# Top-k attention and Fourier mixing on one core: the seven products of the fast block multiply laid into two PSUM banks in turns

## The chip, the core and the metric

The kernel runs on one core of one Trainium2 chip. The metric is the device time of one execution in microseconds (us), as the median of several runs. The core's engines are TensorE (PE in the profile, its weight loads PEld), VectorE (DVE), ScalarE (ACT), GpSimd (POOL) and SyncE (SP, which issues the transfers here). Each engine works through its own list of instructions in order, and waits on semaphores where it needs another engine's result. TensorE writes its results to PSUM, which has eight banks of 128 x 512 float32; VectorE and ScalarE read them from there.

## The reference, cut to what matters

Eight batches, eight heads, 576 tokens, head size 64. The attention keeps the 32 largest scores of each row. Its output, 576 x 512 per batch, goes through a Fourier mix, a normalisation and two matrix products with 2048 hidden channels.

```python
scores = scale * np.matmul(q, k.transpose(0, 1, 3, 2))
kth = np.partition(scores, -top_k, axis=-1)[..., -top_k:-top_k + 1]
scores = np.where(scores >= kth, scores, -1000000000.0)
attn = softmax(scores)                       # cut: max, exp, sum + 1e-9
x = np.matmul(attn, v)                       # then (B,H,S,D) -> (B,S,H*D)

mixed = np.real(fft(fft(x, axis=1), axis=2)).astype(np.float32)
u = x + mixed
un = (u - mean(u)) / np.sqrt(var(u) + 1e-06) # over the last axis
ch = np.maximum(un @ w_ch1, 0.0) @ w_ch2
out = (u + ch).astype(np.float32)
```

## The kernel before

The program is one long loop over steps `i`. A step handles one tile of 128 query rows (36 steps per batch, 288 in all): TensorE makes scores for tile i + 3, transposes the finished tile i - 2 (`tpP`) and multiplies by `v`; VectorE finds the 32 largest of each row with MAX8 and MATCH_REPLACE8; GpSimd turns the 32nd value into bounds (`nt`); ScalarE and GpSimd mask (`wk`), and ScalarE takes the exponential. The mix and the matrix products of the batch before are cut into units and laid between these as TensorE filler: `hidden` units write `hp`, the products of the second matrix are called p1 to p7.

PSUM has four pools: two banks `ps_s` for scores, two `ps_t` for transposes, one `ps_o`, and three `ps_m` that `bank()` hands out in turn. A bank that is held is passed over.

```python
held, turn = set(), [0]
def bank(shape, name, hold=False):
    while turn[0] in held:
        turn[0] = (turn[0] + 1) % 3
    n = turn[0]
    turn[0] = (n + 1) % 3
    t = ps_m.tile(shape, F32, name=name, tag=f"m{n}", bufs=1)
    if not hold:
        return t
    held.add(n)
    return t, lambda: held.discard(n)
```

A bank that isn't held may be handed out while an earlier reader is still to come. TensorE then waits for this reader.

The Fourier mix has three TensorE parts for each batch: four token transforms (`yp`, two for each parity), five channel transforms (`mp`, one per tile of tokens) and five transposes (`tpu`). In all batches but the last they take a bank of the three:

```python
yp = ps_t.tile(shape, F32, name=name, tag="tp") if b == B - 1 else bank(shape, name)
...
mp = ps_s.tile(shape, F32, name=name, tag="sp") if b == B - 1 else bank(shape, name)
...
tp = ps_t.tile(shape, F32, name=name, tag="tp") if b == B - 1 else bank(shape, name)   # tpu
```

The second matrix product is done, for batches 1 to 7, as a block multiply with seven products instead of eight (two row tiles `ta`, `tb`, two halves of the channels), once for each of two chunks `ch` of tokens. Each product is two units of four matmuls of 256 columns. All share two banks, `v` and `w`, with a half (`lo`, `hi`) per result. A product that follows in the same half adds to what stands there. GpSimd makes the sums of blocks of the hidden layer (`mix`), each in two halves.

```python
def p2(part):
    if part == 0:
        mix("21", "21", "22", ALU.add)
    c = product("v", lo, "12", streamed(B21), part, True)
    if part: to_x(ta, lo, c, None if ch else 0)
def p4(part):
    c = product("v", hi, "22", streamed(T4), part, False)
    if part: to_x(tb, lo, c, None if ch else 1); banks["v"][1]()      # bank v given back
def p1(part):
    c = product("w", lo, "11", b11, part, True)
    if part:
        to_x(ta, lo, c, 2)
        mix("11", "21", "11"); mix("12", "12", "11"); mix("22", "22", "11")
def p5(part):
    need((b, ch, ("21", part)))
    c = product("w", hi, "21", streamed(T1), part, False)
    if part: to_x(tb, hi, c, 3)
def p6(part):
    need((b, ch, ("11", part)))
    c = product("w", lo, "11", streamed(T2), part, False)
    if part: to_x(ta, hi, c, 0)
def p3(part):
    need((b, ch, ("12", part)))
    c = product("w", hi, "12", b22, part, False)
    if part: to_x(ta, hi, c, 1); store(ta)
def p7(part):
    need((b, ch, ("22", part)))
    c = product("w", lo, "22", streamed(T3), part, False)
    if part: to_x(tb, slice(0, DM), c, None if ch else 2); store(tb); banks["w"][1]()
# order of the units: p2, p4, p1, p5, p6, p3, p7
```

`to_x` adds a result to `x`. With a place `n`, ScalarE scales it out of PSUM at once and GpSimd adds it later from a list `sums`; with `None`, or in the last batch, VectorE does both in one instruction (line 992). Outside the last batch that instruction is put off by one to two steps (`late_next`), so that it doesn't stand ahead of the top-k work.

GpSimd takes from `sums` once in each step, ahead of the bounds; `need` pulls everything that stands before a wanted key:

```python
run(i, "pool0")
some_sums(max(3.4 - planned, 0.0))      # us of sums in this step
bounds(i)
...
def need(key):
    while key not in summed:
        got, _, fn, _ = sums.pop(0)
        fn()
        summed.add(got)
```

Of the kernel before, what the change touches and what calls it, by code (L numbers as in the profile page):

```python
# [64 lines left out]
def kernel(  # L65
# [544 lines left out]
    def dft_tokens(b, par, g2):  # L610

        while any(u[2] == "hidden" for u in queue):
            one_unit()
        _, zw, fg = folded[b, par]
        if b not in y_of:
            y_of[b] = batp.tile([P, 4, S], F32, name=f"y_{b}", tag="y")
        y = y_of[b]
        shape, name = [P, 2, KQ], f"yp_{b}_{par}_{g2}"

        yp = ps_t.tile(shape, F32, name=name, tag="tp") if b == B - 1 else bank(shape, name)  # L620

        def mm(gg, st, lhsT, rows, table, start=False):

            nc.tensor.matmul(  # L624
                yp[0:rows, gg, :],
                lhsT=lhsT,
                rhs=fs[:, table, par, st, :],
                start=start,
                stop=st == 2,
                skip_group_check=True,  # L630
            )


        for gg in range(2):
            g = 2 * g2 + gg
            for st in range(3):
                f = fg[:, st] if st < 2 else ftail
                mm(gg, st, f[:, P * g:P * (g + 1)], P, gg, start=gg == 0 and st == 0)
        if g2 == 0:
            for st in range(3):  # L640
                mm(1, st, zw[:, st, Q1:Q1 + 1] if st < 2 else ftail[:, DM:DM + 1], 1, 0)

        mir, back = (
            (slice(HS + 2, S, 2), slice(KQ - 2, 0, -1)) if par == 0
            else (slice(HS + 1, S, 2), slice(KQ - 2, None, -1))
        )
        y2 = y[:, 2 * g2:2 * g2 + 2, :]
        nc.scalar.copy(out=y2[:, :, par:HS + 1:2], in_=yp[:, :, 0:KQ - par])
        nc.scalar.copy(out=y2[:, 0, mir], in_=yp[:, 0, back])
        nc.scalar.mul(out=y2[:, 1, mir], in_=yp[:, 1, back], mul=sg[:, g2:g2 + 1])  # L650
        if par == 1 and g2 == 1:
            tails_of_y(b)
        return 2.15
# [6 lines left out]
    def dft_channels(b, t, quick=False):  # L660

        rows, y = ROWS[t], y_of[b]
        shape, name = [P, 2, DM // 2], f"mp_{b}_{t}"
        mp = ps_s.tile(shape, F32, name=name, tag="sp") if b == B - 1 else bank(shape, name)
        for par in range(2):
            for j in range(2):
                g = 2 * par + j
                if t == 4:
                    lhsT = yt_of[b][:, g].rearrange("p h r -> p (h r)")
                else:  # L670
                    k0 = HS * (t // 2) + P * (t % 2)
                    lhsT = y[:, g, k0:k0 + P]
                nc.tensor.matmul(
                    mp[0:rows, par, :], lhsT=lhsT, rhs=fd[:, g, :],
                    start=(j == 0), stop=(j == 1),
                )
        if quick:
            xt = two(x_of[b][0:rows, t, :])
            at(now[0], "dve", lambda: nc.vector.tensor_tensor(
                out=xt, in0=mp[0:rows], in1=xt, op=ALU.add  # L680
            ))
            at(now[0], "dve", lambda: stats(b, t))
            return 1.75
        key = (b, t > 1 and t < 4)
        if key not in us_of:
            us_of[key] = batp.tile(
                [P, 2 if key[1] else 3, DM], F32, name=f"us_{b}_{t}", tag="fold_d" if key[1] else "fold_s"
            )
        us = us_of[key][0:rows, CHUNKS[int(key[1])].index(t), :]
        nc.scalar.copy(out=two(us), in_=mp[0:rows])  # L690
        return 1.75
# [35 lines left out]
    def channels_first(b, t):  # L727

        rows = ROWS[t]
        ch, col = CHUNK_OF[t]  # L730
        if (b, ch) not in unT_of:
            unT_of[b, ch] = batp.tile(
                [P, NDT, CW[0]], F32, name=f"unT_{b}_{ch}", tag="fold_s" if ch == 0 else "y"
            )
        shape, name = [P, NDT, P], f"tpu_{b}_{t}"
        tp = ps_t.tile(shape, F32, name=name, tag="tp") if b == B - 1 else bank(shape, name)
        for dt in range(NDT):
            nc.tensor.transpose(
                tp[:, dt, 0:rows], x_of[b][0:rows, t, P * dt:P * (dt + 1)], ident[0:rows, 0:rows]
            )  # L740
        nc.scalar.copy(out=unT_of[b, ch][:, :, col:col + rows], in_=tp[:, :, 0:rows])
        return 0.6

# [14 lines left out]
    stream = []  # L760
    for _ in range(B - 1):
        for ch in range(2):
            stream += [(o, kc) for o in (B21, T4, T1, T2, T3) for kc in range(NK)]
            if ch == 0:
                stream += [(o, kc) for kc in range(NK) for o in (T1, B21)]
    places = [w2[:, kc, DH:DM] for kc in range(NK)] + [w2[:, NK + kc, 0:DH] for kc in range(NK)]
# [57 lines left out]
            summed.add(key)  # L824

    def need(key):
        while key not in summed:
            got, _, fn, _ = sums.pop(0)
            fn()
            summed.add(got)  # L830

    def mlp_units(b):
# [110 lines left out]
        def fast(ch):  # L945
# [37 lines left out]
                for n in range(2):  # L983
                    later((dst, n), 1.25, lambda n=n: go(NK // 2 * n), True)

            def to_x(t, cols, src, n):

                xt = x[:, t, cols].rearrange("p (e c) -> p e c", c=DH)
                e = xt.shape[1]
                if n is None or last:  # L990
                    def add():
                        nc.vector.scalar_tensor_tensor(  # L992
                            out=xt,
                            in0=src.rearrange("p (e c) -> p e c", e=1).to_broadcast([P, e, DH]),
                            scalar=rs[:, t:t + 1], in1=xt, op0=ALU.mult, op1=ALU.add,
                        )
                    if last:
                        add()
                    else:
                        late_next.append(add)  # L1000
                    return
                r = room(n)
                nc.scalar.mul(out=r, in_=src, mul=rs[:, t:t + 1])
                key = "x", t, cols.start, n
                used[n] = b, ch, key
                rb = r.rearrange("p (e c) -> p e c", e=1)
                later(key, 0.75 * e, lambda: nc.gpsimd.tensor_tensor(
                    out=xt, in0=xt, in1=rb.to_broadcast([P, e, DH]) if e > 1 else rb, op=ALU.add
                ))

            def store(t):
# [7 lines left out]
                if last:  # L1019
                    go()  # L1020
                else:

                    later(("out", t), 0.0, lambda: at(now[0] + 2, "load2", go))

            def half_bank(name, cols):
                if name not in banks:
# [19 lines left out]
            def p2(part):  # L1046
                if part == 0:
                    mix("21", "21", "22", ALU.add)
                c = product("v", lo, "12", streamed(B21), part, True)
                if part:  # L1050
                    to_x(ta, lo, c, None if ch else 0)

            def p4(part):
                c = product("v", hi, "22", streamed(T4), part, False)
                if part:
                    to_x(tb, lo, c, None if ch else 1)
                    banks["v"][1]()

            def p1(part):
                c = product("w", lo, "11", b11, part, True)  # L1060
                if part:
                    to_x(ta, lo, c, 2)
                    mix("11", "21", "11")
                    mix("12", "12", "11")
                    mix("22", "22", "11")

            def p5(part):
                need((b, ch, ("21", part)))
                c = product("w", hi, "21", streamed(T1), part, False)
                if part:  # L1070
                    to_x(tb, hi, c, 3)

            def p6(part):
                need((b, ch, ("11", part)))
# [3 lines left out]

            def p3(part):
                need((b, ch, ("12", part)))  # L1080
                c = product("w", hi, "12", b22, part, False)
                if part:
                    to_x(ta, hi, c, 1)
                    store(ta)

            def p7(part):
                need((b, ch, ("22", part)))
                c = product("w", lo, "22", streamed(T3), part, False)
                if part:
                    to_x(tb, slice(0, DM), c, None if ch else 2)  # L1090
                    store(tb)
                    banks["w"][1]()

            def tails(half, part):
                n = CHUNKS[ch].index(4)
# [17 lines left out]

            units = [
                (1.75, lambda f=f, part=part: f(part), "back")
                for f in (p2, p4, p1, p5, p6, p3, p7) for part in range(2)
            ]
            if ch == 0:
                units += [
# [139 lines left out]
    for b in range(B):  # L1259
# [42 lines left out]
                at(ft[par], "pe1", lambda b=b, par=par, g2=g2: dft_tokens(b, par, g2), 2.15)  # L1302
        for n, t in enumerate((0, 1, 4, 2, 3)):
            quick = first or last
            s = fc + (0 if first else n // 3 if last else n // 2)
            at(s, "pe2", lambda b=b, t=t, q=quick: dft_channels(b, t, q), 1.75)
            if not quick:
                at(s, "pool2", lambda b=b, t=t: add_mixed(b, t))
# [50 lines left out]
    while i < N + 4 or plan or queue or sums:  # L1359
# [98 lines left out]

        planned = 1.5 * len(plan.get((i, "pool0"), [])) + 1.3 * len(plan.get((i, "pool2"), []))
        run(i, "pool0")  # L1460
        some_sums(max(3.4 - planned, 0.0))
        bounds(i)
        if i < PER_BATCH:
            mask(i)
        for fn in late_now:
# [44 lines left out]
```

## Time and profile before

| what | value |
|---|---|
| median of 3 runs | 1973.29 us (1973.12 to 1973.54) |
| span of the profiled run | 1971.8 us |
| VectorE busy | 1588.8 us (81%) |
| ScalarE busy | 1220.0 us (62%) |
| GpSimd busy | 961.9 us (49%) |
| DMA rate over the span | 77 GB/s, hardware queue 26.2% of 16 engines |

Busy is the time in which an engine has an instruction under way. An engine's idle time is put down to what ended it, for example "PE hp L848 <- DVE x L992": TensorE stood before a matmul into `hp` until a VectorE instruction of line 992 that works on `x` was done. "issue" means that the profile shows nothing that it waited for. The granted clock (PEclk) is the share of full TensorE clock that the chip allowed; at 0.5 a matmul takes twice as long.

### The profile page before, as it was taken

To read this page: it belongs to the slowest core of one execution; us is meant where nothing else is said; L and a number is where in the kernel's file an instruction comes from. 1 tells how busy PE (TensorE), PEld (TensorE's weight loads), DVE (VectorE), ACT (ScalarE), POOL (GpSimd) and SP (SyncE) were. 2 spreads that over 40 slices of the span, in tenths; PEclk is the share of its full clock that TensorE was granted. 3 is DMA by queue.
4 is the path that set the end of the run, shared out by engine and by line. 5 is a ranking of instruction groups with operands and counts; after the bars stand their busy time and mean duration, and the time that the engine had idled before them with its cause. 6 is when DMAs were issued, how large, how long until landed. Compare 5 with 4: busy or idle time off the path is not lost.

```text
span 1971.8 us, 30544 instructions
## 1 busy us (share of the span) xinstructions
PE 1803.6 (91%) x9520; PEld 1271.9 (65%) x9520; DVE 1588.8 (81%) x3274; ACT 1220.0 (62%) x3108; POOL 961.9 (49%) x1246
## 2 busy tenths in 40 slices
PE   5566799999999989999999998999799999998998
PEld 3333465465676766777666765767567776777777
DVE  8999989899999989888798877988868888852110
ACT  6878657676876767666676665666656667651100
POOL 4768544546434573546435563446525464344112
PEclk7787899999999999999999998999999999999999
DMA  5323001211224230333114131233203331133151
GB/s 162 111 87 97 19 13 51 86 40 29 62 65 135 62 93 19 105 92 97 50 40 146 52 96 34 82 107 83 66 18 112 86 98 53 46 118 107 43 163 43
DMA packets 235633, 151.37 MB, mean 77 GB/s; under 512 B 135248, under 2 KB 226512, under 8 KB 235472
## 3 DMA queue, kind: packets, MB, share of 16 engines
q1 hardware_dynamic: 234688, 149.22, 26.2%
q8 instruction: 76, 1.25, 0.3%
q14 instruction: 85, 0.70, 0.1%
q10 hardware_dynamic: 784, 0.21, 0.0%
HBM read 134.65 MB, written 14.68 MB: 76 GB/s over the span
## 4 chain that ended last, share of the span: by engine, by line
PE 69%; POOL 12%; DVE 8%; issue 5%; ACT 4%; DMA 0%; SPq 0%; POOLq 0%; DVEq 0%; ACTq 0%
PE hp L848 24%; PE cw L1036 10%; PE o L465 6%; PE sp L363 5%; PE tpP L428 5%; POOL wk L401 4%; PE cv L1036 4%; DVE m L384 3%; PE yp L624 3%; DVE wk L386 3%; PE cp L1105 3%; POOL w L215 2%; POOL w L214 2%; PE cp L872 2%; PE sp_t L333 1%
## 5 line engine op out<-in xcount | busy, mean ns | idle before, releaser
L401 POOL TENSOR_TENSOR wk<-S,wk 128x576 f32<-128x576 f32 x288 | 407.9, 1416 | 764.1 <-ACT wk L400 743.5
L384 DVE MAX8 m<-wk 128x8 f32<-128x576 f32 x864 | 623.0, 748 | 5.2
L848 PE MATMUL hp<-unT,w 128*128 128x256 f32 (+1 forms) x2048 | 544.9, 413 | 13.7 <-DVE x L992 11.6
L848 PEld LDWEIGHTS hp<-unT,w 128*128 128x128 f32 x2048 | 376.8, 192 | 140.4 <-issue 34.3
L386 DVE MATCH_REPLACE8 wk<-m,wk 128x576 f32<-128x576 f32 x576 | 427.5, 742 | 0.0
L1036 PE MATMUL cw<-w,hT 128*128 128x256 f32 x1056 | 256.6, 389 | 26.8 <-POOL hT L980 14.6
L407 ACT ACTIVATE wk<-wk,nt 128x576 f32<-128x576 f32 x288 | 224.7, 780 | 71.4 <-POOL wk L401 70.2
L400 ACT ACTIVATE wk<-S,nt 128x576 f32<-128x576 f32 x288 | 226.9, 788 | 48.5 <-POOL nt L393 47.4
L428 PE MATMUL tpP<-ident,wk 128*128 128x128 f32 x1152 | 183.9, 284 | 73.4 <-ACT wk L407 48.6
L1036 PEld LDWEIGHTS cw<-w,hT 128*128 128x128 f32 x1056 | 193.7, 192 | 72.8 <-issue 25.4
L384 DVE MAX8 m<-S 128x8 f32<-128x576 f32 x288 | 213.9, 743 | 24.1 <-ACT S L337 21.8
L852 ACT ACTIVATE hT<-hp 128x320 f32<-128x320 f32 (+1 forms) x256 | 105.0, 410 | 202.4 <-PE hp L848 200.4
L428 PEld LDWEIGHTS tpP<-ident,wk 128*128 128x128 f32 x1152 | 140.5, 145 | 136.1 <-ACT wk L407 70.1
L431 ACT COPY PT<-tpP 128x512 f32<-128x512 f32 (+1 forms) x320 | 171.1, 546 | 80.0 <-PE tpP L428 77.5
L386 DVE MATCH_REPLACE8 wk<-m,S 128x576 f32<-128x576 f32 x288 | 213.5, 741 | 0.0
L980 POOL TENSOR_TENSOR hT<-hT 128x512 f32<-128x512 f32 x112 | 140.7, 1272 | 124.8 <-ACT hT L852 95.7
L465 PE MATMUL o<-PT,v 128*64 128x256 f32 (+3 forms) x1440 | 195.9, 415 | 1.9 <-ACT PT L431 1.9
L366 ACT COPY S<-sp 128x512 f32<-128x512 f32 (+1 forms) x264 | 141.9, 589 | 49.7 <-PE sp L363 49.6
L363 PE MATMUL sp<-kT,qT 64*128 64x512 f32 (+1 forms) x528 | 159.0, 662 | 4.2 <-ACT means L1234 3.3
L465 PEld LDWEIGHTS o<-PT,v 128*64 128x64 f32 x1440 | 111.5, 153 | 72.2 <-issue 15.7
L1036 PE MATMUL cv<-w,hT 128*128 128x256 f32 x432 | 102.7, 382 | 1.2 <-DVE x L992 1.2
L1036 PEld LDWEIGHTS cv<-w,hT 128*128 128x128 f32 x432 | 78.4, 190 | 16.2 <-issue 4.3
(149 smaller groups left out, 2145.0 us busy)
## 6 DMA issues: line engine op xcount, KB each, us to landing
w<-w_parts SPq DMA_DIRECT2D x624, 128.0 KB, 2.5
space<-in_moe_w_ch_dram SPq DMA_DIRECT2D x32, 512.0 KB, 3.6
nat<-in_q_dram SPq DMA_DIRECT2D x128, 64.0 KB, 2.1
v<-in_v_dram SPq DMA_DIRECT2D x128, 64.0 KB, 2.1
out_dram<-x SPq DMA_DIRECT2D x32, 256.0 KB, 2.1
nat<-in_k_dram SPq DMA_DIRECT2D x124, 64.0 KB, 2.2
w_s<-w_parts SPq DMA_DIRECT2D x48, 128.0 KB, 2.6
w_parts<-w_t SPq DMA_DIRECT2D x8, 512.0 KB, 2.9
```

The costliest lines, as they stand in the source:

```text
L363: nc.tensor.matmul(sp[r], lhsT=qT[hd, q_cols], rhs=kT[hd, :], start=True, stop=True)
L366: nc.scalar.copy(out=s_t[r, keys], in_=sp[r])
L384: ops.append(lambda src=src, m8=m8: nc.vector.max(out=m8, in_=src))
L386: ops.append(lambda src=src, m8=m8: nc.vector.match_replace(w, m8, src, NEG))
L400: nc.scalar.activation(out=w, in_=Ssb[i], func=AF.Relu, scale=-FAR, bias=Nt[i][:, 1:2])
L401: nc.gpsimd.tensor_tensor(out=w, in0=Ssb.pop(i), in1=w, op=ALU.subtract)
L407: nc.scalar.activation(out=w, in_=w, func=AF.Exp, bias=Nt.pop(i)[:, 0:1], accum_out=den_t[pair % 3][:, c:c + 1],)
L428: nc.tensor.transpose(tp[:, c, :], p_sb[:, k0 + P * c:k0 + P * (c + 1)], ident)
L431: nc.scalar.copy(out=pt[:, NF * he:NF * (he + 1), col:col + w], in_=tp[:, :, o:o + w])
L465: nc.tensor.matmul(o[D * e:D * (e + 1), c0:c1], lhsT=vv[:, c, e, :], rhs=pt[:, 2 * NF if c == NF else NF * e + c, c0:c1], start=(c == 0), ...
L848: nc.tensor.matmul(hp[:, 0:w], lhsT=w1[:, dt, P * it:P * (it + 1)], rhs=unT[:, dt, 0:w], start=(dt == 0), stop=(dt == NDT - 1),)
L1036: nc.tensor.matmul(dst, lhsT=h()[a][:, kc, :], rhs=rhs, start=start and kc == 0, stop=kc == NK - 1, skip_group_check=True,)
```

## The change

It regroups the use of PSUM around the seven products, and moves some GpSimd work.

1. The products run in the order p2, p1, p5, p4, p6, p3, p7 and go to the banks v, w, v, w, w, v, w. Before, they went to v, v and then five times to w.
2. Both banks stay held until VectorE's last read of them is in the program: `to_x` takes a `then`, called once that read is emitted. Before, they were given back at once.
3. Of the results of a chunk, p3 and p7 go through VectorE; before it was p2, p4 and p7 in chunk 1 alone.
4. With two of three banks held for longer, half the transforms of batches 2 to 6 go to the two banks of `ps_t`: `yp` with g2 = 1, `mp` of tiles 1 and 2, `tpu` of tiles 0 and 2.
5. For the same batches the channel transforms are spread: one per step and not two.
6. GpSimd takes up to 2.1 us of sums before the bounds and 1.3 us after them; `need` pulls only sums of the wanted kind (mix, or add to x). Stores are planned one step earlier.

```diff
-        yp = ps_t.tile(shape, F32, name=name, tag="tp") if b == B - 1 else bank(shape, name)
+        there = b == B - 1 or b > 1 and g2 == 1
+        yp = ps_t.tile(shape, F32, name=name, tag="tp") if there else bank(shape, name)
...
-        mp = ps_s.tile(shape, F32, name=name, tag="sp") if b == B - 1 else bank(shape, name)
+        if b == B - 1:
+            mp = ps_s.tile(shape, F32, name=name, tag="sp")
+        elif b > 1 and t in (1, 2):
+            mp = ps_t.tile(shape, F32, name=name, tag="tp")
+        else:
+            mp = bank(shape, name)
...
-        tp = ps_t.tile(shape, F32, name=name, tag="tp") if b == B - 1 else bank(shape, name)
+        there = b == B - 1 or b > 1 and t in (0, 2)
+        tp = ps_t.tile(shape, F32, name=name, tag="tp") if there else bank(shape, name)
...
-            stream += [(o, kc) for o in (B21, T4, T1, T2, T3) for kc in range(NK)]
+            stream += [(o, kc) for o in (B21, T1, T4, T2, T3) for kc in range(NK)]
...
     def need(key):
-        while key not in summed:
-            got, _, fn, _ = sums.pop(0)
-            fn()
-            summed.add(got)
+        if key in summed:
+            return
+        kind = next(s[3] for s in sums if s[0] == key)
+        for s in [s for s in sums if s[3] == kind]:
+            sums.remove(s)
+            s[2]()
+            summed.add(s[0])
+            if s[0] == key:
+                break
...
-            def to_x(t, cols, src, n):
+            def to_x(t, cols, src, n, then=lambda: None):
...                     (in the VectorE form, after the instruction)
+                        then()
...                     (store)
-                    later(("out", t), 0.0, lambda: at(now[0] + 2, "load2", go))
+                    later(("out", t), 0.0, lambda: at(now[0] + 1, "load2", go))
...                     (p2)
-                    to_x(ta, lo, c, None if ch else 0)
+                    to_x(ta, lo, c, 0)
...                     (p1)
-                    to_x(ta, lo, c, 2)
+                    to_x(ta, lo, c, 1)
                     mix("11", "21", "11")
                     mix("12", "12", "11")
-                    mix("22", "22", "11")
...                     (p5)
-                c = product("w", hi, "21", streamed(T1), part, False)
+                c = product("v", hi, "21", streamed(T1), part, False)
...                     (p4, now after p5)
-                c = product("v", hi, "22", streamed(T4), part, False)
-                    banks["v"][1]()
+                c = product("w", hi, "22", streamed(T4), part, False)
+                    to_x(tb, lo, c, 3)
+                    mix("22", "22", "11")
...                     (p3, p7)
-                c = product("w", hi, "12", b22, part, False)
-                    to_x(ta, hi, c, 1)
-                    store(ta)
+                c = product("v", hi, "12", b22, part, False)
+                    to_x(ta, hi, c, None, lambda: (banks["v"][1](), store(ta)))
-                    to_x(tb, slice(0, DM), c, None if ch else 2)
-                    store(tb)
-                    banks["w"][1]()
+                    to_x(tb, slice(0, DM), c, None, lambda: (banks["w"][1](), store(tb)))
...
-                for f in (p2, p4, p1, p5, p6, p3, p7) for part in range(2)
+                for f in (p2, p1, p5, p4, p6, p3, p7) for part in range(2)
...
-            s = fc + (0 if first else n // 3 if last else n // 2)
+            s = fc + (0 if first else n // 3 if last else n // 2 if soon else n)
...
-        some_sums(max(3.4 - planned, 0.0))
+        some_sums(max(2.1 - planned, 0.0))
         bounds(i)
+        some_sums(1.3)
```

## The prediction

> **What bounds the kernel now.** I read the busy shares first, then the stages, then TensorE's waits in the stage that the change touches, and last the timeline around the longest of them.
>
> ```profile
> PE 1803.6 (91%) x9520; PEld 1271.9 (65%) x9520; DVE 1588.8 (81%) x3274; ACT 1220.0 (62%) x3108; POOL 961.9 (49%) x1246
> PEclk7787899999999999999999998999999999999999
> ```
>
> TensorE is the busiest, and the change takes no matmul from it. The 1804 us stay, so what can be won is TensorE's idle time and the time it runs at a lower clock. The view by stages says where that is (columns: stretch, its us, then busy us of PE, PEld, DVE, ACT, POOL, then the granted clock, the DMA share and GB/s):
>
> ```profile
> 0.00:500.00 500.00, 400.47 (x1958) 245.49 (x1958) 462.67 (x951) 355.90 (x900) 283.42 (x344) 0.89 0.24 69
> 500.00:690.00 190.00, 188.63 (x1062) 134.77 (x1061) 186.33 (x387) 139.87 (x362) 92.33 (x127) 1.00 0.30 83
> 690.00:1760.00 1070.00, 1019.52 (x5580) 735.31 (x5580) 908.90 (x1885) 690.16 (x1762) 533.51 (x708) 0.98 0.27 78
> 1760.00:1972.00 212.00, 194.99 (x929) 156.36 (x924) 30.92 (x53) 34.09 (x86) 52.64 (x67) 0.98 0.27 83
> ```
>
> Of 168 us idle, 500 - 400 = 100 lie before 500 us, in batch 0, where the seven products aren't in use yet: out of reach. The first product runs at 570 us. From 690 on there are 1070 - 1019.5 = 50.5 us (batches 2 to 6), and 212 - 195 = 17 us in the last stage. TensorE's waits between 690 and 1760 us (total, times, longest):
>
> ```profile
> PE cw L1036 <- POOL hT L980: 14.6, 11, 2.2
> PE hp L848 <- DVE x L992: 11.6, 2, 8.2
> PE tpu L738 <- DVE x L992: 9.2, 2, 7.4
> PE cw L1036 <- issue: 4.1, 10, 1.0
> ```
>
> 20.8 of the 50.5 us are four waits for VectorE's put-off read of a bank (L992), and 14.6 us are products that wait for GpSimd's block sums. The longest, on TensorE's timeline and then VectorE's:
>
> ```profile
> 1421.78 0.39 PE L333 MATMUL sp_t<-kt,qT 128*128 128x128 f32 x2
> 1430.40 4.47 PE L848 MATMUL hp<-unT,w 128*128 128x320 f32 x8 [8.23 <-DVE x L992]
> 1436.40 2.42 PE L848 MATMUL hp<-unT,w 128*128 128x320 f32 x8
> ```
>
> ```profile
> 1429.60 0.74 DVE L992 SCALAR_TENSOR_TENSOR x<-cw,gi,x 128x512 f32<-128x512 f32 x1
> ...
> 1442.12 0.18 DVE L492 RECIPROCAL rd<-rd 128x4 f32<-128x4 f32 x1 [3.67 <-ACT rd L491]
> ...
> 1452.77 0.42 DVE L509 TENSOR_TENSOR x<-tpx,rd 128x256 f32<-128x256 f32 x1 [5.04 <-PE tpx L505]
> ```
>
> The first hidden unit was handed the bank of p7, whose reader stands behind a tile and more of top-k work. TensorE stood for 8.23 us; then VectorE in turn idled for 3.67 and 5.04 us on things that TensorE made late. It is a ring, so this time isn't hidden on the other side. And the eight matmuls after the wait took 4.47 us against 2.42 for the same eight later.
>
> **What the Trainium skill says.** "TensorE: Matmul & The Clock Gate", section "What's actually happening": the array drops to half clock after an idle window of about 3.4 us and returns after a busy one. The trace agrees for the 8.23 us wait (clock 0.50 in the stage from 1430.4 to 1434.5), but goes further: matmuls are slow after waits of only 2.23 us too (eight `cw` matmuls 2.73 us at 931.69, against 1.89 elsewhere). "PSUM — Partial Sum Buffer", section "PSUM bank collisions raise a hardware error": two engines may not be in one bank and quadrant at once, so guard by bank, not by address. The trace agrees: in the last batch a product into the other half of the same bank still stands about 0.62 us for the read of the half before, a read of 0.48 us. "Perfetto Trace Analysis", "Optimization Strategy": the same gap repeating can mean too little PSUM; here the 2.23 us gap repeats in each batch (929, 1156, 1384, 1618 us), but its cause is GpSimd.
>
> **Part by part.**
>
> A. *Banks held until VectorE's read (point 2).* With `v` and `w` passed over, neither `hp` nor `tpu` can be handed a bank with a late reader. The four waits, 20.8 us, lose their cause. Around them, though, VectorE works without a gap for some 35 us (1397 to 1432), so a part will come back as a wait for the exponential ahead of `tpP` (1.95 us of that stand at 1465 already). I count 0.7 x 20.8 = 14.6 us.
>
> B. *Order of products and split of the sums (points 1, 6).* The 2.23 us gap is p3 waiting for the sum "12". In the new order p4 stands between p5 and p6, so "11" and "12" have two units (2 x 1.73 us) more. The sum after the bounds uses a hole: at 929.01 the mask on GpSimd had waited 2.53 us for ScalarE while three block sums (3.73 us together) stood behind it. Against: "21" has two units less. I count 0.65 x 14.6 = 9.5 us.
>
> C. *Banks in turns (point 1).* The last batch, where products follow each other with nothing between:
>
> ```profile
> 1892.02 3.69 PE L1036 MATMUL cw<-w_s,hT 128*128 128x256 f32 x16 [0.62 <-issue]
> 1896.38 3.69 PE L1036 MATMUL cw<-w,hT 128*128 128x256 f32 x16 [0.67 <-DVE x L992]
> 1900.70 1.53 PE L1036 MATMUL cw<-w,hT 128*128 128x256 f32 x6 [0.62 <-issue]
> ```
>
> Such waits sum to 4.4 + 1.3 + 1.2 = 6.9 us on 11 places after 1760 us. In v, w, v, w, w, v, w one pair of six still meets in one bank (p4 to p6), where it was five of six; about a quarter stays. Gain 5 us. In the stage before, the "issue" waits on `cw` (4.1 us) and one of 2.0 us for ScalarE are of this kind, half go: 3 us.
>
> D. *Clock.* The clock record has six half-clock stretches in 690 to 1760 us, four of 3.4 us and two of 10.2, each beginning within 3 us of the start of one of the waits of A or B, or of the 1.95 us one. Leaving out what lies inside the waits, TensorE worked at half clock for about 4 x 3.4 + 5.0 + 4.1 = 22.7 us, which costs half, 11.3. Two thirds go with their waits: 7.3 us.
>
> Sum of gains: 14.6 + 9.5 + 5 + 3 + 7.3 = 39.4 us.
>
> E. *New costs.* A `yp` in `ps_t` is read by three ScalarE instructions (0.42 + 0.29 + 0.41, about 1 us overlapped). `tpP_t`, the second transpose after it, gets that bank again: at 901.84 it would have waited until 902.48, 0.6 us. Two such `yp` per batch, 5 batches, 6 us if all meet, about 4 as only every second tile has a `tpP_t`. `mp` and `tpu` have one read of 0.6 us each: 2 us in all. With both banks held only one is left for `hp`, tails and the other transforms: two hidden units in a row in one bank wait for the ReLU, 0.42 us and its signal, unless other work lies between; 3 us. The batch's units arrive two steps later (five channel transforms over five steps), which shifts work and may idle TensorE at the seam: 2 us. VectorE gets 2 x (0.48 + 0.75) = 2.46 us per batch instead of 1.7; six batches, under 5 us on an engine that has 161 idle in the stage: nothing. ScalarE and GpSimd have less to do: nothing. Sum 11 us.
>
> Net: 39.4 - 11 = 28.4 us. 1973.3 - 28.4 = 1944.9, so **1945 us**.
>
> **Rivals.** *VectorE becomes the bound.* It is busy 909 of 1070 us (85%), and stretches around the transforms have no hole. If TensorE, freed of its waits for banks, only waits ahead of `tpP` for the next exponential, A and its share of D vanish: 39.4 - 14.6 - 4 - 11, some 10 us of gain, 1963. For it: no idle VectorE time from 1397 to 1432. Against it: VectorE idles right after the wait, for TensorE's sake.
> *One bank is too few.* With two held over 14 units, everything else of three banks runs through one, and `ps_t` has the transposes of the attention on the critical path too. If each `yp`, `mp`, `tpu` and some hidden units wait 0.6 to 1 us, 14 per batch x 0.8 x 5 = 56 us are lost, and the kernel ends at 1985 to 1995. Against it: the channel transforms are now one per step, and ScalarE is only 62% busy.
> *All of it is gained.* Every wait and half-clock stretch goes and the new ones hide: 20.8 + 14.6 + 6.9 + 6 + 11.3 = 60 us at most, 1914.
>
> **Range and chances.** The rivals' ends, 1914 and 1990, need everything to go one way. The middle of what I hold likely is 1930 to 1963, and I widen it a little on both sides: 1926 to 1967. Over 2% faster means under 1933.8, which takes 40 us net, all of my gains at no cost: 0.22. Over 2% slower means 2012.8 or more: 0.02, as even the crowded-bank rival stays below. Within 2%: 0.76.
>
> **What would show it.** Right if "hp" and "tpu" no longer wait for DVE x L992 (A), if "cw <- POOL hT" falls from 14.6 to about 5 us (B), if the last stage's idle falls from 17 to about 12 us (C), and if the clock in 690 to 1760 is 0.99 (D). E shows as waits of `tpP_t`, `tpP`, `yp` or `hp` for ScalarE (hT, y, us, unT), about 10 us. Wrong, if TensorE's wait "tpP <- ACT wk", 3.4 us in this stage now, grows past 20: then VectorE is the bound. Wrong as well, if `hp` waits for ScalarE's hT in many small pieces: then the banks are too few.

## The result, and the profile after

The changed kernel takes 1960.5 us (median of 4 runs, 1952.7 to 1961.1) against 1973.4 us: a ratio of 0.9925, 95% interval 0.990 to 0.995. It is faster by 13 us. The prediction was 1945, with a range of 1926 to 1967: the sign is right, and the gain is less than half of the 28 us that its sum gave.

The page after, engines and granted clock:

```profile
PE 1804.9 (92%) x9520; PEld 1275.4 (65%) x9520; DVE 1589.6 (81%) x3280; ACT 1215.3 (62%) x3102; POOL 951.8 (49%) x1240
PEclk8787899999999999999999999999999999999999
```

TensorE's busy time is the same within 1.3 us, so its share rose because the span shrank. The same stages as before (us, then busy us of PE, PEld, DVE, ACT, POOL, granted clock, DMA share, GB/s):

```profile
690.00:1760.00 1070.00, 1027.39 (x5606) 741.41 (x5605) 910.08 (x1892) 687.62 (x1762) 526.08 (x704) 0.99 0.28 79
1760.00:1959.00 199.00, 189.70 (x906) 155.22 (x904) 29.18 (x49) 31.64 (x80) 50.70 (x66) 0.98 0.29 88
```

TensorE is idle for 42.6 us in the long stage, where it was 50.5, and for 9.3 in the last, where it was 17. What it waits for in the long stage has changed altogether (line numbers have moved: VectorE's read is L1007, GpSimd's block sum L994):

```profile
PE cv L1052 <- POOL hT L994: 19.2, 8, 2.9
PE mp L679 <- ACT qT L285: 6.3, 4, 1.6
PE tpP_t L439 <- ACT unT L748: 5.4, 5, 2.4
PE tpP_t L439 <- ACT y L651: 4.7, 9, 0.5
PE mp L679 <- ACT PT L431: 2.4, 5, 0.5
```

No wait for VectorE's put-off read is left; it was 20.8 us. The waits for GpSimd grew from 14.6 to 20.4 us (19.2 on `cv`, 1.2 on `cw`). The other four lines, 18.8 us, are new: transforms and transposes that meet in the two banks of `ps_t` and wait for ScalarE's read of a bank. Summed over everything after 500 us, the idle time between TensorE's instructions fell from 64.6 to 50.9 us. That is 13.7 us, for 13.4 us between the spans (1971.8 to 1958.4).

In the last batch, banks in turns do what they were meant to. One wait of 0.62 us is left in each chunk, where p6 follows p4 in `w`:

```profile
1884.06 3.69 PE L1052 MATMUL cw<-w,hT 128*128 128x256 f32 x16 [0.62 <-issue]
1887.58 3.62 PE L1052 MATMUL cv<-w,hT 128*128 128x256 f32 x16
1891.04 3.62 PE L1052 MATMUL cw<-w,hT 128*128 128x256 f32 x16
```

And this is the costliest of the new waits, on TensorE's timeline:

```profile
1188.97 0.33 PE L439 MATMUL tpP_t<-ident,wk 128*128 128x128 f32 x1 [0.64 <-ACT unT L748]
...
1189.46 0.77 PE L277 MATMUL tpq<-ident,nat 128*128 128x128 f32 x5
1191.79 3.59 PE L679 MATMUL mp<-fd,y 128*128 128x256 f32 x8 [1.57 <-ACT qT L285]
...
1196.78 1.99 PE L679 MATMUL mp<-fd,y 128*128 128x256 f32 x8
```

The transposes of q (`tpq`, four and one) have just taken both banks of `ps_t`; `mp` of tile 2 wants one and stands for ScalarE's copy. Its eight matmuls then take 3.59 us where the next eight take 1.99: a half-clock stretch. The wait recurs in four batches, the stretch in two of them.

### The profile page after: what moved, and what is told of

Its sections match the earlier page's. It is cut to its first block, busy times and chain, and to the rows that moved or that the text cites. A ratio compares the mean times of both kernels' runs of the same rounds, so it can differ in the third digit from the quotient of the medians.

```text
span 1958.4 us, 30524 instructions
## 1 busy us (share of the span) xinstructions
PE 1804.9 (92%) x9520; PEld 1275.4 (65%) x9520; DVE 1589.6 (81%) x3280; ACT 1215.3 (62%) x3102; POOL 951.8 (49%) x1240
## 4 chain that ended last, share of the span: by engine, by line
PE 72%; POOL 10%; ACT 7%; DVE 6%; issue 4%; DMA 0%; SPq 0%; POOLq 0%; ACTq 0%; DVEq 0%
PE hp L862 25%; PE cw L1052 8%; PE o L465 6%; PE cv L1052 6%; PE sp L363 5%; PE tpP L428 5%; POOL wk L401 3%; PE yp L625 3%; DVE m L384 3%; PE cp L1117 3%; PE mp L679 3%; DVE wk L386 2%; PE cp L886 2%; PE sp_t L333 1%; ACT wk L407 1%
## 5 line engine op out<-in xcount | busy, mean ns | idle before, releaser
L401 POOL TENSOR_TENSOR wk<-S,wk 128x576 f32<-128x576 f32 x288 | 407.0, 1413 | 760.9 <-ACT wk L400 703.3
L862 PE MATMUL hp<-unT,w 128*128 128x256 f32 (+1 forms) x2048 | 536.6, 409 | 2.1 <-ACT unT L748 2.1
L384 DVE MAX8 m<-S 128x8 f32<-128x576 f32 x288 | 213.9, 743 | 17.9 <-ACT S L337 15.9
L994 POOL TENSOR_TENSOR hT<-hT 128x512 f32<-128x512 f32 x112 | 142.0, 1273 | 130.7 <-ACT hT L866 92.4
L1052 PE MATMUL cw<-w,hT 128*128 128x256 f32 x840 | 200.8, 384 | 2.9 <-issue 1.2
L1052 PE MATMUL cv<-w,hT 128*128 128x256 f32 x656 | 161.9, 395 | 19.2 <-POOL hT L994 19.2
L1052 PEld LDWEIGHTS cw<-w,hT 128*128 128x128 f32 x840 | 153.8, 191 | 38.1 <-issue 12.5
L363 PE MATMUL sp<-kT,qT 64*128 64x512 f32 (+1 forms) x528 | 165.5, 666 | 5.2 <-ACT means L1246 3.3
L366 ACT COPY S<-sp 128x512 f32<-128x512 f32 (+1 forms) x264 | 141.8, 589 | 43.6 <-PE sp L363 43.4
L1052 PEld LDWEIGHTS cv<-w,hT 128*128 128x128 f32 x656 | 124.8, 197 | 47.7 <-POOL hT L994 24.4
```

The source lines that it names most:

```text
L363: nc.tensor.matmul(sp[r], lhsT=qT[hd, q_cols], rhs=kT[hd, :], start=True, stop=True)
L384: ops.append(lambda src=src, m8=m8: nc.vector.max(out=m8, in_=src))
L401: nc.gpsimd.tensor_tensor(out=w, in0=Ssb.pop(i), in1=w, op=ALU.subtract)
L862: nc.tensor.matmul(hp[:, 0:w], lhsT=w1[:, dt, P * it:P * (it + 1)], rhs=unT[:, dt, 0:w], start=(dt == 0), stop=(dt == NDT - 1),)
L994: nc.gpsimd.tensor_tensor(out=v[dst][:, k], in0=v[a][:, k], in1=v[c][:, k], op=op)
L1052: nc.tensor.matmul(dst, lhsT=h()[a][:, kc, :], rhs=rhs, start=start and kc == 0, stop=kc == NK - 1, skip_group_check=True,)
```

## The experiments

The theory after the result: the hold is the gain, and two other parts of the change pay some of it back, the move to `ps_t` and the closer order around GpSimd's sums. Two measures are read beside each time: TensorE's idle time after 500 us, between its instructions, and the length of the half-clock stretches after 500 us by the trace's clock record, up to the end of the span. The spans lie between 1912 and 1983 us; the span less the idle time and half of these stretches is 1884 to 1895 us in all fourteen kernels, so the two explain the rest within 11 us. The runs were made on several chips, each time with the kernel before beside them (medians 1972.7 to 1973.9 us). A ratio is to these runs, by means; where two changed kernels are compared, one or two us may be the chip's.

| kernel | us | ratio to before, 95% | idle | half clock |
|---|---|---|---|---|
| before | 1973 | | 64.6 | 45.8 |
| changed | 1960.5 | 0.9925 (0.990 to 0.995) | 50.9 | 30.7 |
| hold alone | 1942.1 | 0.9849 (0.9836 to 0.9861) | 43.9 | 23.0 |
| move to `ps_t` alone | 1985.3 | 1.0056 (1.0043 to 1.0069) | 70.5 | 47.8 |
| changed, no hold | 1977.2 | 1.0018 (1.0010 to 1.0025) | 60.1 | 51.2 |
| changed, transforms back | 1948.5 | 0.9878 (0.9865 to 0.9891) | 49.2 | 13.7 |
| changed, `mp` 1 and 3 | 1946.2 | 0.9863 (0.9847 to 0.9878) | 47.6 | 13.7 |
| changed, sums all ahead | 1955.5 | 0.9925 (0.9900 to 0.9949) | 50.7 | 51.2 |
| changed, p4 ahead of p5 | 1954.5 | 0.9906 (0.9893 to 0.9919) | 43.6 | 30.7 |
| changed, 2.6 us behind | 1930.6 | 0.9785 (0.9766 to 0.9804) | 30.9 | 13.7 |
| back and p4 first | 1944.2 | 0.9850 (0.9831 to 0.9868) | 43.1 | 17.9 |
| the same, 2.6 us behind | 1921.9 | 0.9741 (0.9727 to 0.9754) | 28.5 | 10.2 |
| hold, 2.6 us behind | 1927.6 | 0.9767 (0.9748 to 0.9786) | 32.0 | 10.9 |
| best, two transforms a step | 1915.0 | 0.9707 (0.9688 to 0.9727) | 24.6 | 6.8 |

### The hold alone

```diff
 (kernel before; to_x takes `then`, called after VectorE's instruction or ScalarE's)
-                    to_x(tb, lo, c, None if ch else 1)
-                    banks["v"][1]()
+                    to_x(tb, lo, c, None if ch else 1, lambda: banks["v"][1]())
...
-                    to_x(tb, slice(0, DM), c, None if ch else 2)
-                    banks["w"][1]()
+                    to_x(tb, slice(0, DM), c, None if ch else 2, lambda: banks["w"][1]())
```

> The kernel before with one thing changed: a bank of the seven products that VectorE will read stays held until that read is in the program. Order of products, transforms and sums as before. Theory (the bank waits were a real cost): the four waits of hp and tpu for VectorE's line 992 (20.8 us) are gone, TensorE's idle between 690 and 1760 us falls by 15 to 20 us, half-clock time falls too, and the time is 1950 to 1958 us. Rival (VectorE is the bound around the transforms): the waits come back ahead of tpP as waits for the exponential, over 15 us of them, and the time stays within 5 us of 1973.

1942.1 us: 31 us less than before, and 18 less than the whole change. The waits in the long stage:

```profile
PE cw L1038 <- POOL hT L980: 14.6, 11, 2.2
PE cw L1038 <- issue: 3.9, 9, 1.0
PE tpP L428 <- ACT wk L407: 3.4, 3, 1.9
```

Against the list before, the two lines with VectorE are gone and the others are as they were, "tpP" at 3.4 us too: nothing came back. Idle fell by 20.7 us, the full sum of the four waits; half-clock stretches fell by 23 us, of which those inside the old waits were idle anyway. The theory's mechanism holds, and its 1950 to 1958 us counted too little. The rival (VectorE is the bound) falls.

### The hold taken out of the changed kernel

```diff
-                    to_x(ta, hi, c, None, lambda: (banks["v"][1](), store(ta)))
+                    to_x(ta, hi, c, None, lambda: store(ta))
+                    banks["v"][1]()
 (the same for p7 and "w")
```

> The changed kernel with both banks given back at once after p3 and p7, as before, and not after VectorE's read. Theory (the hold is what brings the gain): waits of TensorE for VectorE's line 1007 of 12 to 30 us come back and the time is 1972 to 1992 us. Rival (banks in turns and fewer transforms in the three banks avoid the late reader on their own): under 6 us of such waits, time within 6 us of 1960.

1977.2 us: slower than before by 0.2%. The hold is the gain in this setting too. But the waits for VectorE are smaller than the theory had it, 9.8 us on two places:

```profile
PE mp L679 <- DVE x L1007: 5.6, 1, 5.6
PE tpu L745 <- DVE x L1007: 4.2, 1, 4.2
```

Idle rose by 9.2 us, and the half-clock stretches by 20.5; both together give 9.2 + 10.2 = 19 us, for 17 measured.

### The move to ps_t alone

```diff
 (kernel before, with the change's three edits to where yp, mp and tpu lie, and nothing else)
```

> The kernel before with the move of half the transforms of batches 2 to 6 to ps_t alone; no hold, order and sums as before. Theory (the move costs by itself): waits of tpP_t and mp for ScalarE of 15 to 20 us appear, the waits of hp for VectorE's line 992 stay at 10 us or more, the time is 1976 to 1992 us. Rival (the move is a second way to the gain, as fewer transforms are handed a bank with a late reader): the waits for line 992 fall by over 15 us, and the time is 1958 to 1970 us.

1985.3 us, 11 to 12 more than before and in the theory's range; the rival falls. But two of the theory's numbers were wrong. Of the 15 to 20 us of waits of `tpP_t` and `mp` for ScalarE, only 4.8 + 1.4 = 6.2 us came, all of `tpP_t`. And `hp` waits only 4.0 us for VectorE: the late reader now meets `tpu` more often, and the sum is 22.6 us:

```profile
PE tpu L745 <- DVE x L999: 18.6, 3, 8.9
PE tpP_t L439 <- ACT y L651: 4.8, 9, 0.5
PE hp L855 <- DVE x L999: 4.0, 1, 4.0
```

Taking half of the users away doesn't take the late reader out of the turn. The move is no second way to the gain. The 18.8 us of waits at `ps_t` in the changed kernel are not the move's alone: there the channel transforms also come one per step and not two (point 5). No run puts that one point back in the changed kernel, so its share is not shown.

### The transforms back in banks of their own

```diff
-        there = b == B - 1 or b > 1 and g2 == 1
+        there = b == B - 1
...
-        elif b > 1 and t in (1, 2):
+        elif False:
...
-        there = b == B - 1 or b > 1 and t in (0, 2)
+        there = b == B - 1
```

> The changed kernel with the transforms of batches 2 to 6 (yp, mp, tpu) back in the three banks of their own; all else as changed. Theory (the move to the banks of the attention's transposes costs more than it saves): the 18.8 us of waits of tpP_t and mp for ScalarE go, some waits of the second yp for the copies out of the first come (two per batch, about 1.2 us, 12 us in five batches), and the time is 1948 to 1960 us. Rival (one free bank is too few, so the move is needed for the hold): waits for ScalarE's y, us, unT and hT grow to over 30 us and the time is 1965 us or more.

1948.5 us, 12 below the changed kernel: the move isn't needed for the hold, and costs. But hardly through the length of its waits. The idle time is nearly the same, 49.2 us: the 18.8 us at `ps_t` are gone, and 18.5 us in small pieces stand in their place (`tpP` for the exponential 6.1, where it was 2.0; `yp` for ScalarE 4.8, `tpq` 4.1, `mp` 1.9, a transfer of weights 1.6). The 1.9 us of `mp` are a wait for VectorE's put-off read again: the hold ends when that read is in the program, not when it is done. What differs is the half-clock time, 13.7 us for 30.7, worth 8.5 of the 12. Here too only a part is owed to waits that went: the waits for GpSimd are the same 20.4 us, yet fewer stretches follow them.

### Another tile's transform in ps_t

```diff
-        elif b > 1 and t in (1, 2):
+        elif b > 1 and t in (1, 3):
```

> The changed kernel with mp of tiles 1 and 3, not 1 and 2, in ps_t: tile 2 falls in the step in which the transposes of q take both banks of ps_t. Theory (the wait of mp for ScalarE's qT and the half-clock stretch after it are the costly part of the move): mp's waits of 6.3 us go, the eight matmuls of 3.59 us after it are back at 1.99, and the time is 1946 to 1955 us. Rival (small waits cost no more than their length): 6 us less at most, 1954 or more.

1946.2 us. With one number changed, `mp` no longer falls into the step of `tpq`; the matmuls after it are at full speed:

```profile
1185.99 0.77 PE L277 MATMUL tpq<-ident,nat 128*128 128x128 f32 x5
1186.59 1.89 PE L679 MATMUL mp<-fd,y 128*128 128x256 f32 x8
```

6.3 us of waits went, 3.3 us of others came (`tpP_t` for ScalarE's `us`): idle fell by 3.3 us, half-clock by 17.0, together 3.3 + 8.5 = 12 of the 14 us measured. The time is where the theory had it and outside the rival's range, but the cause is only half shown. Of the stretches that went, two had stood behind `mp` (6.8 us); two more had stood behind waits for GpSimd that are still there and have none now, and the one behind `yp` in the last stage is shorter by 3.4 us. So 3.3 + 3.4 = 7 us belong to the placement of `mp`, and the rest to where the half-clock stretches fall.

### GpSimd's sums all ahead of the bounds

```diff
-        some_sums(max(2.1 - planned, 0.0))
+        some_sums(max(3.4 - planned, 0.0))
         bounds(i)
-        some_sums(1.3)
```

> The changed kernel with GpSimd's sums all ahead of the bounds again (3.4 us of them less what is planned, nothing behind). Theory (the split brought little, as either way one block sum per step is made while the transforms' sums are planned): time within 6 us of the changed kernel's 1960, the waits of the products for GpSimd between 15 and 25 us. Rival (the split is where the gain comes from): the waits for GpSimd rise over 30 us or ScalarE's mask waits longer for the bounds, and the time is 1968 us or more.

1955.5 us, with an interval that covers the changed kernel's; the waits for GpSimd are 18.9 us against 20.4. The split by itself brings nothing. (The profiled run of this kernel took 1972.6 us, with the changed kernel's idle time but 20 us more at half clock, where its other five took 1955.0 to 1955.9; the table's half-clock number is of that run, and the ratio takes it in.)

### p4 ahead of p5

```diff
-            stream += [(o, kc) for o in (B21, T1, T4, T2, T3) for kc in range(NK)]
+            stream += [(o, kc) for o in (B21, T4, T1, T2, T3) for kc in range(NK)]
...
-                for f in (p2, p1, p5, p4, p6, p3, p7) for part in range(2)
+                for f in (p2, p1, p4, p5, p6, p3, p7) for part in range(2)
```

> The changed kernel with p4 put back ahead of p5 (order p2, p1, p4, p5, p6, p3, p7, banks v, w, w, v, w, v, w, and the weights streamed in that order). Theory (p5 stands too close behind the sum 21 that it needs): the 2.3 us waits of the second half of p5, one per batch, go with the half-clock stretch after each, the waits for GpSimd fall from 20.4 to about 11 us, and the time is 1946 to 1954 us. Rival (GpSimd's rate of one block sum per step is what counts): the wait moves on to p6 or p3, the sum of waits for GpSimd stays at 18 us or more and the time at 1957 or more.

1954.5 us. The waits for GpSimd fall to 11.7 us on four places, all of p3, and idle by 7.3 us: the mechanism is as the theory had it. The time lies half a microsecond outside its range, since the half-clock stretches didn't go (30.7 us in both): one after each of the four remaining waits of 2.9 us, and after three of the four of `mp`.

### More sums behind the bounds

```diff
         bounds(i)
-        some_sums(1.3)
+        some_sums(2.6)
```

GpSimd's timeline in the changed kernel, around a wait of p3 (1157.0 to 1159.9 us on TensorE), shows why:

```profile
1151.49 0.18 POOL L393 TENSOR_TENSOR nt<-m,cc 128x2 f32<-128x2 f32 x1
1151.64 1.28 POOL L994 TENSOR_TENSOR hT<-hT 128x512 f32<-128x512 f32 x1
1156.52 1.40 POOL L401 TENSOR_TENSOR wk<-S,wk 128x576 f32<-128x576 f32 x1 [3.61 <-ACT wk L400]
```

After the bounds (L393) it makes one block sum, as 1.3 us allow no second, and then stands for 3.61 us before the mask (L401), while p3's sum waits behind that. The slot was first widened on top of a kernel that has both repairs from above, transforms back and p4 ahead of p5. That kernel itself, still with 1.3 us:

> The changed kernel with the transforms back in the three banks of their own and p4 ahead of p5 as well. Theory (the two losses are separate and add): TensorE's idle after 500 us falls from 49 us (transforms back alone) to about 40, and the time is 1937 to 1945 us. Rival (another wait takes the place of the one for the sum 21): idle stays over 46 us and the time over 1946.

1944.2 us, idle 43.1, within the theory's range: the two repairs together give 4 us over the transforms alone (the intervals overlap), though idle fell by 6.1. Then with 2.6 us:

> As the kernel with transforms back and p4 ahead of p5, and GpSimd may make 2.6 us of sums behind the bounds, not 1.3 (two block sums in the hole ahead of the mask). Theory (GpSimd stands 2.3 to 3.6 us before the mask for ScalarE while block sums wait behind it): the last 2.9 us waits of p3 for the sum 12 go, the waits of TensorE for GpSimd are under 4 us, idle after 500 us is about 30 us, and the time is 1925 to 1936 us. Rival (the longer sums delay the mask, so the exponential and tpP): waits of tpP for ScalarE's wk rise over 10 us and the time is 1937 or more.

1921.9 us, better than the theory's range. The same place:

```profile
1142.55 0.21 POOL L393 TENSOR_TENSOR nt<-m,cc 128x2 f32<-128x2 f32 x1
1142.69 2.53 POOL L994 TENSOR_TENSOR hT<-hT 128x512 f32<-128x512 f32 x2
1145.16 1.43 POOL L401 TENSOR_TENSOR wk<-S,wk 128x576 f32<-128x576 f32 x1
```

Two sums fill the hole and the mask follows at once. No wait of TensorE for GpSimd is left in the stage, and `tpP` waits 5.6 us for the exponential, where it was 6.1. Then by itself, on the changed kernel:

> The changed kernel with one number changed: 2.6 us of GpSimd's sums behind the bounds, not 1.3. Theory (the products wait for block sums only because one sum per step is made while GpSimd waits for ScalarE): TensorE's waits for GpSimd fall from 20.4 to under 4 us, those at ps_t (19 us) stay, idle after 500 us is about 32 us and the time 1934 to 1944 us. Rival (the waits at ps_t hide part of it): idle over 40 us, time 1946 or more.

1930.6 us: 30 us less than the changed kernel by one number, and 3 below the theory's range. Idle fell by the 20 us expected; half-clock stretches went from 30.7 to 13.7 us, and only one of the four long waits of `mp` is followed by one. The number also raises what GpSimd may sum in one step, from 3.4 to 4.7 us. No run allows 4.7 us ahead of the bounds, so that the place in the hole counts, and not the amount, is read from the timeline and not shown by a run. And on the hold alone, with all else as in the kernel before:

> The kernel before with the hold, and the sums as 2.1 us ahead of the bounds and 2.6 us behind; order of the products and transforms as before. Theory (hold and sums are nearly all; the order in turns brings only the short waits within one bank): the 14.6 us of waits for GpSimd fall under 4 us, about 13 us of waits within one bank stay, and the time is 1924 to 1931 us, 2 to 9 us above the best so far. Rival (the new order is needed for the sums to be in time): waits for GpSimd stay over 8 us and the time is 1934 or more.

1927.6 us, a time as expected: of the waits for block sums 1.1 us are left, with 3.1 us for other work of GpSimd. The hold and the slots on GpSimd are 45 us of gain without a new order or any move. The order with p4 ahead of p5, VectorE's new reads and the rest of the change, with the transforms in their own banks, bring 6 us more (1921.9).

### Two channel transforms per step again

```diff
-            s = fc + (0 if first else n // 3 if last else n // 2 if soon else n)
+            s = fc + (0 if first else n // 3 if last else n // 2)
```

> The best kernel so far (transforms in their own banks, p4 ahead of p5, 2.6 us of sums behind the bounds; 1921.9 us) with the channel transforms two per step again, not one. Theory (with two of three banks held, one is left, so two in one step meet in it): waits of mp and tpu for ScalarE of 6 us or more appear, time 1928 to 1938 us. Rival (the units between keep them apart, and they arrive two steps sooner): time within 4 us of 1922.

1915.0 us on top of the 1921.9: the fastest kernel of the study. My theory missed, and so did the rival's range. The waits of `mp` and `tpu` for ScalarE did appear, 5.8 us, but more went:

```profile
PE mp L679 <- ACT us L696: 4.3, 3, 1.4
PE yp L625 <- ACT y L651: 4.0, 4, 1.0
...
PE tpq L277 <- ACT PT L431: 2.1, 5, 0.5
PE tpP L428 <- ACT wk L407: 2.0, 3, 1.1
```

"tpq" had 5.8 and "tpP" 5.6 us before. That the units arrive two steps sooner and fill these places is a guess; no run parts it from the rest. What is shown is that point 5 of the change costs 7 us in this setting. Without it, the new order, the reads and the rest are worth 12.6 us over the hold and the slots (1927.6), and not 6.

## Why the prediction was right in sign and short in size

Against the sum, A brought about 6 us more and C 4 more; B brought 15 less, D 6 less, and E cost 8 more. That is some 19 us less on balance, for 15.5 measured. That the time still fell into the range owes something to luck: the two gains that were counted too low hid part of what B, D and E missed.

**A, the hold (14.6 us expected).** Right in mechanism, and the size too small: 20.7 us of idle went in the run with the hold alone, and the time fell by 31 us. I had kept back 30% for VectorE, which had no hole for 35 us before the wait. It is still not the bound: its own 3.67 and 5.04 us of idle after the wait, seen before, were slack, and no new wait of `tpP` came.

**B, the order and the sums (9.5 us expected).** This step failed, and it is the largest part of the shortfall: waits for GpSimd rose by 5.8 us, a term wrong by 15. I saw that "21" had two units less and gave it no number. It cost 2.3 us in three batches and 0.6 in one, and p4 put back ahead of p5 removed that. And "12" didn't gain from its two extra units (2.9 us, where it was 2.2), for units aren't what sets it: while the transforms' folds are planned, 2.1 less the planned 1.5 us leaves room for no sum ahead of the bounds, and 1.3 us for one behind them. One sum per step was the rate before, too. I read the hole in front of the mask rightly, and did not check that the new slot was too short to use it for two sums.

**C, banks in turns (8 us expected).** Right in mechanism, and counted low: the cw and cv waits of the last stage fell from 6.9 to 1.2 us, 5.7 for 5 expected, and in the stage before "issue" and ScalarE's 6.1 us went, for 3.

**D, the clock (7.3 us expected).** It came only where nothing else spoiled it. The reading was a little short: the long stage has seven half-clock stretches, five of 3.4 us and two of 10.2, and TensorE worked for 25.7 us in them, not 22.7. Only half clock under TensorE's work costs time. After 500 us that was 30.4 us before, 17.7 with the hold alone (worth about 6 us) and 28.4 in the changed kernel (worth 1 us). In the changed kernel the new waits of `mp` and of the products brought their own stretches.

**E, the costs (11 us expected).** The move to `ps_t` was put at 6 us. Alone it made 6.2 us of waits, in the changed kernel 18.8. For `yp` the 0.6 us were right (nine waits of 0.5). What I did not have in the sum is that q's transposes take both banks in the step of tile 2, and that a wait of 1.6 us can cost as much again in clock (eight matmuls 3.59 us for 1.99). For a single free bank I had 3 us, on `hp`: it doesn't wait, and with the transforms back `yp` waits 4.8. The 2 us for the later units are not parted; two per step is 7 us faster.

**The rivals.** VectorE as the bound is refuted by the hold alone. "One bank is too few" is refuted by the transforms back. "All of it is gained" (1914 us) was dismissed as a bound that needs everything at once. The best kernel, 1915.0, comes within 1 us of it, but by a wider slot on GpSimd and an order that the change doesn't have, so the agreement is chance.

## What to carry to other kernels

A rotating buffer with one late reader on another engine stalls the writer in order; here, keeping the bank out of the rotation until that reader is in the program was worth 31 us, though it leaves one bank of three for a time. When work on a helper engine is late, look for the hole in front of its next wait and size the slot to the hole, before reordering the consumers. A change in several parts should be measured part by part: here one part alone made 31 us, and the others together gave back 18 of them, some of it by chance of the clock.

## What was not expected of the hardware

The Trainium skill ("TensorE: Matmul & The Clock Gate", "What's actually happening") has the clock halved after an idle window of about 3.4 us. Here half-clock stretches of 3.4 us followed much shorter waits: 1.57 us with one of 0.64 shortly before it (the changed kernel, 1191.8 us), and single waits of 2.2 to 2.9 us. It doesn't follow each of them. With the transforms back, two of the seven waits of products for GpSimd over 2 us had one after them; in the run with the sums all ahead, each such wait had one. This parts kernels of nearly equal idle time by 8 us.

The traces show what decides most of it. In all fourteen, the clock record changes only at points of a grid of 3.413 us. Take TensorE's idle time in each interval of this grid that lies after 500 us and has the full clock, 5804 in all. Of the intervals with more than 2.01 us idle, 69 of 69 were followed by half clock; of those with less than 1.72 us, none of 5708; in between, 16 of 27. (From 100 to 500 us the border is less sharp: 14 of 150 half-clock intervals that follow a full one come after less.) So it counts how much of a wait falls into one interval. With the transforms back, the 2.31 us wait for GpSimd at 1361.9 us has 2.28 us in one, and a stretch follows; the longer wait at 1380.5 us, 2.92 us, has 1.96 us in one and 0.96 in the next, and none follows. The clock came back to full after half-clock intervals with up to 0.50 us idle (85 of 85), and stayed at half after 0.66 us or more (21 of 21).

The grid lies differently against the start of the program in each trace (one of its points lies 0.39 us after it in the changed kernel, 2.30 us in the one with the sums ahead). So a shift of the same waits by a microsecond can add or remove stretches. That this also made the 17 us between one run of the kernel with the sums ahead and its other runs is likely but not shown, as only that run's trace is kept.
